# Seven PSUM banks as one tile, and the read-back of a unit's maxima issued nearer to its write, in an attention and gated-MLP block

## The chip, the cores and the metric

The kernel runs on one core of one Trainium2 chip. The metric is device time in microseconds (us) of one execution. A core has TensorE (PE; its weight loads are shown apart as PEld), VectorE (DVE), ScalarE (ACT), GpSimd (POOL) and SyncE (SP), each with its own in-order stream of instructions, and DMA queues. PSUM is the memory that matmuls write; here it is used as eight banks of 128 partitions by 512 fp32.

## The reference

Multi-query attention (32 query heads, one key and one value head of 16 dimensions) and a gated MLP follow each other on 2048 tokens of 512 features, each behind a layer norm and with a residual:

```python
def _A_ref(x, wq, wk, wv, wo):                    # B, S, D, H = 1, 2048, 512, 32; Dh = 16
    q = (x @ wq).reshape(B, S, H, Dh).transpose(0, 2, 1, 3)
    k = x @ wk
    v = x @ wv
    scores = jnp.einsum("bhqd,bkd->bhqk", q, k) * (Dh ** -0.5)
    p = _softmax(scores, axis=-1)
    o = jnp.einsum("bhqk,bkd->bhqd", p, v)
    return o.transpose(0, 2, 1, 3).reshape(B, S, H * Dh) @ wo
def _B_ref(x, W_gate, W_up, W_down):              # F = 1792
    gate, up = x @ W_gate, x @ W_up
    return (gate * (gate > 0) * up) @ W_down
h = x + _A_ref(_layernorm(x), A_wq, A_wk, A_wv, A_wo)
h2 = h + _B_ref(_layernorm(h), B_W_gate, B_W_up, B_W_down)
```

## The kernel before, in words

All is fp32. Where fp32 accuracy is wanted from single-pass matmuls, an operand is split into a rounded part and the rest, and three matmuls add up (`PASSES`, line 262).

Attention is cut into 32 units: 256 tokens of 8 heads each. A unit needs two sweeps over all keys. The first finds each row's maximum score: `max_mm` (line 611) makes one matmul of 512 columns into a bank (L619) and one VectorE reduction of that bank to 128 numbers (`mpart`, L621). A unit has 64 of them. `max_finish` (line 623) then takes the maximum, splits and transposes it, writes it to DRAM (`c_dram`, L638) and reads it back from there into two rows of the unit's queries (`qaug`, L642). The second sweep, `score_mm` (line 652), multiplies keys by these queries (L658), so that the maximum is subtracted on the way, and ScalarE takes exp of the bank into `p` (L661). `value_block` (line 665) multiplies probabilities by values into a bank of its own, "O" (L674); it waits for no B bank.

Layer norms, projections and the MLP are accumulation chains (`Chain`, line 268). Inside the attention each chain matmul is run as two halves of 64 rows (L297), which fill the PE array's rows between the attention's matmuls; a chain keeps one B bank from its first matmul to its last and is then read by ACT, by DVE or by both. The seven banks B0 to B6 are shared by all: `bank()` (line 190) asks the pool for a new tile with the tag of the bank that the planner has chosen, so each use of a bank is a tile of its own.

The order of all this on TensorE, and with it on all engines, is written out by hand: a string `ORDER` of letters (line 49), read by the loop that starts at line 1176. `m`/`M` is a `max_mm` on the lower or upper 64 rows, `e`/`E` a `score_mm`, `g`/`G` one half matmul of a chain, `O` a value block, `T` a turn (transposes). A planner of estimated clocks beside it chooses the bank and the time from which side work (`at`, line 207) is issued. In the program each matmul's reader is written down right behind the matmul, and only then comes the next matmul. The tile layer adds the waits: it records what each instruction reads and writes of each tile, and puts semaphore waits where it finds a conflict.

Of the kernel before, what the change touches and what calls it, by code (L numbers as in the profile page):

```python
# [16 lines left out]
S, D, H, DH, F = 2048, 512, 32, 16, 1792  # L17
# [9 lines left out]
STEPS = NB * 2  # L27
NP = 10
BANKS = [f"B{i}" for i in range(7)]
# [8 lines left out]
PASS, LOAD, SEEN, CHANGE, VALUE, BACK, TURN = 230, 107, 425, 95, 882, 237, 214  # L38

EXP, EXP_FREE, RED, RED_FREE, COPY, ADD, FREE = 494, 650, 600, 740, 541, 600, 150  # L40
ROUND, DIFF, PRODUCT, SCALE, HOP, ISSUE = 640, 1290, 1150, 640, 2600, 600
APPLY, LANDING, ASKED, SPREAD, RAW_LAG = 705, 4700, 5500, 5600, 1500


A_AT, V_AT, P_AT, QUERIES_AT, KEYS_AT, LN_AT = 1800, 1500, 3900, 0, 0, (0, 3000, 2500)

# [110 lines left out]
def block_kernel(ctx: ExitStack, tc: tile.TileContext, x, wq, wkv, wo, wgu, wd, out):  # L157
    nc = tc.nc
    pool = lambda name, **kw: ctx.enter_context(tc.tile_pool(name=name, bufs=1, **kw))
    consts = pool("consts")  # L160
    sb = pool("sb")
    ps = pool("ps", space=PSUM)
# [3 lines left out]
    ident = consts.tile([128, 128], F32, name="ident")  # L166
# [7 lines left out]
    kaug = consts.tile([128, S], F32R, name="kaug")  # L174
# [11 lines left out]


    rota = {"n": 0, "tags": []}

    def bank(tag=None):  # L190
        if tag is None:
            tag = rota["tags"][rota["n"] % len(rota["tags"])]
            rota["n"] += 1
        return ps.tile([128, 512], F32, name=tag, bufs=1)


    clk = {"A": 0.0, "V": 0.0, "P": 0.0, "S": 0.0}
# [388 lines left out]
    qaug = {}  # L586
# [21 lines left out]

    mpart = {}

    def max_mm(m, ab, tag):

        v, i = divmod(m, STEPS)
        j, p, c = i // 8, i // 4 % 2, i % 4
        if v not in mpart:
            mpart[v] = sb.tile([128, 2, 2, 4, 4], F32, name="mpart", bufs=2)
        r = slice(64 * ab, 64 * ab + 62)
        b = bank(tag)
        nc.tensor.matmul(b, qaug[v][r, p, c * 128:(c + 1) * 128], kaug[r, j * 512:(j + 1) * 512],  # L619
                         start=True, stop=True)  # L620
        nc.vector.tensor_reduce(mpart[v][:, ab, p, c, j:j + 1], b, axis=AX.X, op=ALU.max)  # L621

    def max_finish(v):

        m = sb.tile([128, 2, 8], F32, name="mfin", bufs=2)
        nc.vector.tensor_reduce(m.rearrange("p a n -> p (a n)"), mpart.pop(v).rearrange("p a q c j -> p (a q c) j"),
                                axis=AX.X, op=ALU.max)

        ms = sb.tile([128, 2, 2, 8], F32, name="msplit", bufs=2)
        nc.vector.tensor_copy(ms[:, :, 0].bitcast(F32R), m)  # L630
        nc.vector.tensor_tensor(ms[:, :, 1], m, ms[:, :, 0], op=ALU.subtract)

        mt = sb.tile([128, 32], F32, name="mturned", bufs=2)
        nc.vector.transpose(mt, ms.rearrange("p a l n -> p (a l n)"))
        t = on("V", 0.0, 950) + FREE

        def written():
            nc.sync.dma_start(out=c_dram[v], in_=mt)  # L638

        def landed():  # L640
            for ab in range(2):
                nc.sync.dma_start(out=qaug[v][64 * ab + 62:64 * ab + 64].bitcast(F32)  # L642
                                  .rearrange("l q (c i j) -> l (q c) i j", i=4, j=32),
                                  in_=c_dram[v].rearrange("(i a l n) j -> a l n i j", i=4, a=2, l=2)[ab])
            stamp["rows", v] = t + 2 * HOP

        at(t, written)
        at(t + HOP, landed)

    probs = {}  # L650

    def score_mm(g, ab, tag):

        v, i = divmod(g, STEPS)
        kb, p = divmod(i, 2)
        r = slice(64 * ab, 64 * ab + 64)
        b = bank(tag)
        nc.tensor.matmul(b, kaug[r, kb * 128:(kb + 1) * 128], qaug[v][r, p, :], start=True, stop=True)  # L658
        if g not in probs:
            probs[g] = sb.tile([128, 2, T], F32, name="p", bufs=NP)  # L660
        nc.scalar.activation(probs[g][:, ab], b, AF.Exp, scale=DH ** -0.5)  # L661

    obank, osb = {}, {}

# [242 lines left out]
    N = len(UNITS) * STEPS  # L907
# [16 lines left out]
    warm = bank("O")  # L924
# [118 lines left out]
    clk.update(A=A_AT, V=V_AT, P=P_AT, S=0.0)  # L1043
    stamp.update({("xnT", 0, k): 0.0 for k in range(KT)})
    stamp["key", 0], stamp["ln", 1] = KEYS_AT, LN_AT[0]
    end_o, end_t = None, False

    def normalise(t):
# [127 lines left out]
    while not done():  # L1176
# [33 lines left out]
        tag = next_bank() if free else None  # L1210
        starts = {}
        for k in range(2):
            g, w, c = ge[k], me[k], (low, high)[k]
            if g < N and ("rows", g // STEPS) in stamp and g - NP < 2 * on_ and tag:
                starts["eE"[k]] = place(k, max(stamp["rows", g // STEPS], bfree[tag]))
            if w < N and w // STEPS in qtime and w // STEPS <= maxed + 1 and tag and (
                    w >= STEPS or ("key", w // 8) in stamp):
                starts["mM"[k]] = place(k, max(qtime[w // STEPS], bfree[tag], stamp["key", w // 8] if w < STEPS else 0.0))
            if c is not None and (c.tag or tag):
                starts["gG"[k]] = place(k, max(c.t, 0.0 if c.tag else bfree[tag]) if c.i == 0 else 0.0)  # L1220
        top = max(lanes)
        if on_ < N // 2 and len(exps.get(2 * on_ + 1, ())) == 2:
            dep = max(max(exps[g].values()) for g in range(2 * on_, 2 * on_ + 2)) + FREE
# [26 lines left out]
        if any(x.ready() + CHANGE <= top and (x.ready() + 4000 < top or on_ == N // 2) for x in turns):  # L1250
            do_turns()
            continue
        letter = next(order)
        if letter == "T":
            if pending in turns:
                turns.remove(pending)
            for source in (fronts, feeds):
                if source.held is pending:
                    source.held = None
            turn_now(pending, tag, False, end_t)  # L1260
            continue
        kind, k = letter.upper(), int(letter.isupper())
        issued = s = starts[letter]
# [89 lines left out]
```

## Time and profile before

| | us |
|---|---|
| median of 3 runs (1733.37 to 1734.95) | 1734.67 |
| the profiled execution | 1735.53 |
| its span, from first to last instruction | 1733.8 |
| mean granted TensorE clock, share of full | 0.994 |

The profile gives, for one execution, the busy time of each engine, groups of equal instructions by source line (count, sum, mean in ns, idle time ahead of them and who ended it), the waits by pairs of engines, the timeline, and busy time and granted clock in chosen stretches. `B<-kaug,qaug` is a matmul that writes a bank B from `kaug` and `qaug`; the numbers of buffers are left out.

### The profile page before, as it was taken

To read this page: it belongs to the slowest core of one execution; us is meant where nothing else is said; L and a number is where in the kernel's file an instruction comes from. 1 tells how busy PE (TensorE), PEld (TensorE's weight loads), DVE (VectorE), ACT (ScalarE), POOL (GpSimd) and SP (SyncE) were. 2 spreads that over 40 slices of the span, in tenths; PEclk is the share of its full clock that TensorE was granted. 3 is DMA by queue.
4 is the path that set the end of the run, shared out by engine and by line. 5 is a ranking of instruction groups with operands and counts; after the bars stand their busy time and mean duration, and the time that the engine had idled before them with its cause. 6 is when DMAs were issued, how large, how long until landed. Compare 5 with 4: busy or idle time off the path is not lost.

```text
span 1733.8 us, 40138 instructions
## 1 busy us (share of the span) xinstructions
PE 1712.0 (99%) x15566; PEld 1141.9 (66%) x15566; DVE 1451.0 (84%) x2524; ACT 1251.2 (72%) x2488; POOL 854.0 (49%) x1015
## 2 busy tenths in 40 slices
PE   8999999999999999999999999999999999999999
PEld 6755334766656666666766667666666666666688
DVE  8899999988998888988888888897898888986266
ACT  7478977777777777777777777777767777778724
POOL 5511301666415656286544667276655557276410
PEclk9999999999999999999999999999999999999999
DMA  3323211332212222233222223232223223122343
GB/s 129 92 74 86 77 32 26 97 95 79 83 58 72 75 79 81 71 96 97 77 61 83 77 87 99 72 103 70 79 69 108 77 79 102 48 87 81 107 138 116
DMA packets 101970, 144.07 MB, mean 83 GB/s; under 512 B 27156, under 2 KB 39572, under 8 KB 101780
## 3 DMA queue, kind: packets, MB, share of 16 engines
q1 hardware_dynamic: 100724, 141.19, 27.4%
q8 instruction: 122, 2.00, 0.5%
q14 instruction: 68, 0.56, 0.1%
q10 hardware_dynamic: 1056, 0.33, 0.1%
HBM read 119.73 MB, written 21.49 MB: 81 GB/s over the span
## 4 chain that ended last, share of the span: by engine, by line
PE 93%; DVE 5%; issue 1%; DMA 1%; ACT 0%; POOL 0%; SPq 0%; POOLq 0%; DVEq 0%; ACTq 0%
PE B L297 27%; PE O L674 27%; PE B L658 16%; PE B L619 16%; PE B L288 4%; DVE mpart L621 4%; PE B L514 1%; PE O L926 1%; PE B L404 0%; DVE msplit L630 0%; PE B L1001 0%; DMA c_dram<-mturned 0%; DVE hn L397 0%; DMA qaug<-c_dram 0%; PE B L581 0%
## 5 line engine op out<-in xcount | busy, mean ns | idle before, releaser
L621 DVE TENSOR_REDUCE mpart<-B 128x1 f32<-128x512 f32 x2048 | 1268.8, 682 | 190.6 <-PE B L619 111.6
L661 ACT ACTIVATE p<-B 128x512 f32<-128x512 f32 x2048 | 1091.0, 606 | 359.8 <-PE B L658 200.3
L619 PE MATMUL B<-kaug,qaug 62*128 62x512 f32 x2048 | 746.6, 421 | 8.3 <-DVE hT L566 2.6
L658 PE MATMUL B<-qaug,kaug 64*128 64x512 f32 x2048 | 713.6, 417 | 5.6 <-DMA qaug<-c_dram 3.6
L297 PE MATMUL B<-hn,gu 64*128 64x256 f32 x4704 | 564.8, 282 | 0.0
L297 PEld LDWEIGHTS B<-hn,gu 64*128 64x128 f32 x4704 | 533.9, 186 | 24.6 <-issue 15.6
L674 PE MATMUL O<-p,vv 128*32 128x512 f32 x4096 | 510.4, 601 | 0.0
L619 PEld LDWEIGHTS B<-kaug,qaug 62*128 62x128 f32 x2048 | 348.3, 185 | 157.7 <-DVE mpart L621 52.7
L658 PEld LDWEIGHTS B<-qaug,kaug 64*128 64x128 f32 x2048 | 337.6, 186 | 164.7 <-DVE mpart L621 53.4
L869 POOL TENSOR_TENSOR hf<-hf,ga 128x256 f32<-128x256 f32 x92 | 67.4, 733 | 426.0 <-ACT hf L867 417.7
L297 PE MATMUL B<-wd,hT 64*128 64x512 f32 x1176 | 274.6, 395 | 0.1
L240 POOL TENSOR_TENSOR gu<-wraw,gu 128x512 fp32r<-128x512 f32 x195 | 252.9, 1297 | 16.3
L674 PEld LDWEIGHTS O<-p,vv 128*32 128x32 f32 x4096 | 99.8, 109 | 192.0 <-issue 175.5
L297 PEld LDWEIGHTS B<-wd,hT 64*128 64x128 f32 x1176 | 192.0, 185 | 15.3 <-issue 2.7
L240 POOL TENSOR_TENSOR wd<-wraw,wd 128x512 fp32r<-128x512 f32 x95 | 122.4, 1289 | 7.9
L239 POOL TENSOR_SCALAR gu<-wraw 128x512 fp32r<-128x512 f32 x195 | 120.8, 619 | 11.1 <-PE B L297 8.0
L297 PE MATMUL B<-wo,act 64*128 64x512 f32 x384 | 88.3, 394 | 0.1
L240 POOL TENSOR_TENSOR hT<-hf,hT 128x256 fp32r<-128x256 f32 x97 | 72.9, 752 | 8.1
L357 POOL TENSOR_TENSOR rs<-ve,nhalf 128x2 f32<-128x2 f32 (+1 forms) x13 | 10.2, 783 | 125.5 <-DVE nm L353 125.4
L861 ACT ACTIVATE ga<-B 128x256 f32<-128x256 f32 x112 | 43.5, 388 | 39.0 <-PE B L288 24.6
L297 PEld LDWEIGHTS B<-wo,act 64*128 64x128 f32 x384 | 62.6, 185 | 5.5 <-issue 1.7
L528 POOL TENSOR_TENSOR act<-raw,act 128x512 fp32r<-128x512 f32 x16 | 20.6, 1290 | 89.4 <-ACT raw L527 85.7
(134 smaller groups left out, 916.3 us busy)
## 6 DMA issues: line engine op xcount, KB each, us to landing
wraw<-wgu SPq DMA_DIRECT2D x224, 256.0 KB
wraw<-wd SPq DMA_DIRECT2D x112, 256.0 KB
q_dram<-act SPq DMA_DIRECT2D x32, 256.0 KB
qaug<-q_dram SPq DMA_DIRECT2D x62, 128.0 KB
o_dram<-osb SPq DMA_DIRECT2D x31, 256.0 KB
x<-x SPq DMA_DIRECT2D x16, 256.0 KB
out<-h SPq DMA_DIRECT2D x16, 256.0 KB
qaug<-q_dram SPq DMA_DIRECT2D x62, 64.0 KB
```

Of the source, the lines that this page charges most:

```text
L239: nc.gpsimd.tensor_scalar(dst[:, 0], src, 1.0, 0.0, op0=ALU.mult, op1=ALU.add)
L240: nc.gpsimd.tensor_tensor(dst[:, 1], src, dst[:, 0].bitcast(F32), op=ALU.subtract)
L288: nc.tensor.matmul(out(self.bank), l(a), r(b), start=i == 0, stop=i == len(self.ops) - 1)
L297: mm = nc.tensor.matmul(out(self.bank), l(a)[rows], r(b)[rows], start=opens and which == 0, stop=closes and which == 1)
L528: nc.gpsimd.tensor_tensor(qs[:, 1], q, qs[:, 0].bitcast(F32), op=ALU.subtract)
L619: nc.tensor.matmul(b, qaug[v][r, p, c * 128:(c + 1) * 128], kaug[r, j * 512:(j + 1) * 512], start=True, stop=True)
L621: nc.vector.tensor_reduce(mpart[v][:, ab, p, c, j:j + 1], b, axis=AX.X, op=ALU.max)
L658: nc.tensor.matmul(b, kaug[r, kb * 128:(kb + 1) * 128], qaug[v][r, p, :], start=True, stop=True)
L661: nc.scalar.activation(probs[g][:, ab], b, AF.Exp, scale=DH ** -0.5)
L674: nc.tensor.matmul(obank[v][32 * h:32 * h + 32], vv[:, kb, :], probs[g + p][:, ab], start=kb == 0, stop=kb == NB - 1)
L861: nc.scalar.activation(ga[:, :n], p[:, :n], AF.Relu)
L869: nc.gpsimd.tensor_tensor(hf[:, :n], hf[:, :n], ga[:, :n], op=ALU.mult)
```

## The change

Two things are changed that reach the program. The read-back of the maxima is due `ROWS_HOP` = 1700 planned nanoseconds behind the write, where it was `HOP` = 2600; the planned time of its landing stays 5200 (`ROWS_AT`, before 2 x `HOP`). And the seven B banks are one tile of 128 x 7 x 512, allocated once; `bank()` returns a slice of it. The rest adds letters that read two neighbouring banks with one instruction (`X`, `P`), a letter that waits (`W`), a way to finish maxima on GpSimd and warming matmuls: `POOL_ROWS` is 0, `WARMERS` is False, and `ORDER`, which is the same string in both, has none of the three letters, so none of this is in the program.

```diff
+ROWS_HOP, ROWS_AT = 1700, 5200
+POOL_ROWS = 0
+WARMERS = False
...
     rota = {"n": 0, "tags": []}
+    banks = ps.tile([128, len(BANKS), 512], F32, name="B", bufs=1)
...
-        return ps.tile([128, 512], F32, name=tag, bufs=1)
+        return banks[:, BANKS.index(tag)] if tag in BANKS else ps.tile([128, 512], F32, name=tag, bufs=1)
...
-    def max_mm(m, ab, tag):
+    def max_mm(m, ab, tag, pair=None):
...
+        for h in (ab, 1 - ab) if pair is not None else (ab,):
+            r = slice(64 * h, 64 * h + 62)
+            b = bank(tag) if pair is None else banks[:, pair + h]
+            nc.tensor.matmul(b, qaug[v][r, p, c * 128:(c + 1) * 128], kaug[r, j * 512:(j + 1) * 512],
+                             start=True, stop=True)
+        if pair is None:
+            nc.vector.tensor_reduce(mpart[v][:, ab, p, c, j:j + 1], b, axis=AX.X, op=ALU.max)
+        else:
+            nc.vector.tensor_reduce(mpart[v][:, :, p, c, j], banks[:, pair:pair + 2], axis=AX.X, op=ALU.max)
...
-            stamp["rows", v] = t + 2 * HOP
+            stamp["rows", v] = t + ROWS_AT
 
         at(t, written)
-        at(t + HOP, landed)
+        at(t + ROWS_HOP, landed)
```

The order of the instructions on PE, DVE, ACT and POOL is the same in both programs. What differs there is what they wait for.

On PE, in the middle of the program (a gate and up chain beside the two sweeps), before: L658 and L619 are the sweeps' matmuls, L297 the halves of a chain, the number behind B is the bank and the one behind _ the use of it.

```order
L297 MATMUL B2_10585<-hn_7613,gu_10085 128x256 x2
L658 MATMUL B6_10717<-qaug1_76,kaug_78 128x512 [waits DVE_49]
L297 MATMUL B2_10585<-hn_7612,gu_10088 128x256 x2
L619 MATMUL B5_10723<-kaug_78,qaug2_77 128x512 [waits Activation_49]
L297 MATMUL B2_10585<-hn_7612,gu_10088 128x256 x2
L658 MATMUL B0_10728<-qaug1_76,kaug_78 128x512 [waits DVE_49]
L297 MATMUL B2_10585<-hn_7612,gu_10088 128x256
L619 MATMUL B1_10733<-kaug_78,qaug2_77 128x512 [waits Activation_49]
L297 MATMUL B2_10585<-hn_7612,gu_10088 128x256
```

The same place now (L683 was L658, L627 was L619, L303 was L297):

```order
L683 MATMUL B_87<-qaug1_76,kaug_78 128x512
L303 MATMUL B_87<-hn_6261,gu_8348 128x256 [waits Activation_49]
L303 MATMUL B_87<-hn_6261,gu_8348 128x256
L627 MATMUL B_87<-kaug_78,qaug2_77 128x512
L303 MATMUL B_87<-hn_6261,gu_8348 128x256 [waits DVE_49]
L303 MATMUL B_87<-hn_6261,gu_8348 128x256
L683 MATMUL B_87<-qaug1_76,kaug_78 128x512
L303 MATMUL B_87<-hn_6261,gu_8348 128x256 [waits Activation_49]
L627 MATMUL B_87<-kaug_78,qaug2_77 128x512
L303 MATMUL B_87<-hn_6261,gu_8348 128x256 [waits DVE_49]
```

The wait has moved from the sweep's matmul, which waited for the last reader of its own bank, to the instruction behind it: the next chain matmul, in another bank, waits for ACT behind each score matmul and for DVE behind each maximum matmul. The counts that these waits compare with, in the two built programs, say for which instruction: before, 3916 of the 4555 waits of a matmul for an instruction of ACT or DVE name one that read a matmul 9 to 24 places back on PE; now 4093 of 4425 name the reader of the matmul one place back.

On DVE, in the middle of the program, before (the reductions of `mpart`; L893 adds a chain's bank to `h`):

```order
L621 TENSOR_REDUCE mpart_7827<-B6_8601 128x1 [waits PE_49]
L621 TENSOR_REDUCE mpart_7827<-B3_8610 128x1 [waits PE_49]
L621 TENSOR_REDUCE mpart_7827<-B0_8619 128x1 [waits PE_49]
L621 TENSOR_REDUCE mpart_7827<-B1_8631 128x1 [waits PE_49]
L621 TENSOR_REDUCE mpart_7827<-B3_8634 128x1 [waits PE_49]
L621 TENSOR_REDUCE mpart_7827<-B0_8645 128x1 [waits PE_49]
```

The same place now:

```order
L630 TENSOR_REDUCE mpart_6436<-B_87 128x1 [waits PE_49,Activation_49] x4
L630 TENSOR_REDUCE mpart_6436<-B_87 128x1 [waits PE_49]
L630 TENSOR_REDUCE mpart_6436<-B_87 128x1 [waits PE_49,Activation_49]
L921 TENSOR_TENSOR h_5875<-B_87,h_5875 128x512 [waits PE_49,Pool_49]
L630 TENSOR_REDUCE mpart_6436<-B_87 128x1 [waits PE_49,Activation_49] x2
```

A second wait, for ACT's last read of any bank, has come to 1039 of the 2048 reductions; the second of two waits stands in an instruction of its own ahead of the reduction (DVE has 1227 such instructions where it had 180, ACT 1505 where it had 940).

On SP, where unit 2's maxima are written and read back, before and now (in five other units it passes one or two transfers, in 26 none):

```order
L638 DMA c_dram<-mturned 128x32
L431 DMA wraw<-wo 128x1x512 x4
L431 DMA wraw<-wgu 128x512 x4
L642 DMA qaug_77<-c_dram 2x32x32 x2
L226 DMA q_dram<-act 8x16x512 x2
```

```order
L662 DMA c_dram<-mturned 128x32
L666 DMA qaug_77<-c_dram 2x32x32 x2
L437 DMA wraw<-wo 128x1x512 x4
L437 DMA wraw<-wgu 128x512 x4
L232 DMA q_dram<-act 8x16x512 x2
```

The read-back (L642, now L666) has moved ahead of eight loads of weights.

More of the change, by code (lines that the diff above doesn't have):

```diff
@@ L40 @@
 EXP, EXP_FREE, RED, RED_FREE, COPY, ADD, FREE = 494, 650, 600, 740, 541, 600, 150
+EXP_TWO, RED_TWO = 860, 1134
+ROWS_HOP, ROWS_AT = 1700, 5200
+POOL_ROWS = 0
+WARMERS = False
 ROUND, DIFF, PRODUCT, SCALE, HOP, ISSUE = 640, 1290, 1150, 640, 2600, 600
@@ L616, in max_mm @@
             mpart[v] = sb.tile([128, 2, 2, 4, 4], F32, name="mpart", bufs=2)
[L617 to L621, printed above, removed]
+        for h in (ab, 1 - ab) if pair is not None else (ab,):
[3 more added lines that the diff above has]
+                             start=True, stop=True)
@@ L623, in max_finish @@
+        if pair is None:
+            nc.vector.tensor_reduce(mpart[v][:, ab, p, c, j:j + 1], b, axis=AX.X, op=ALU.max)
+        else:
+            nc.vector.tensor_reduce(mpart[v][:, :, p, c, j], banks[:, pair:pair + 2], axis=AX.X, op=ALU.max)
     def max_finish(v):
         m = sb.tile([128, 2, 8], F32, name="mfin", bufs=2)
-        nc.vector.tensor_reduce(m.rearrange("p a n -> p (a n)"), mpart.pop(v).rearrange("p a q c j -> p (a q c) j"),
-                                axis=AX.X, op=ALU.max)
@@ L629, in max_finish @@
         ms = sb.tile([128, 2, 2, 8], F32, name="msplit", bufs=2)
-        nc.vector.tensor_copy(ms[:, :, 0].bitcast(F32R), m)
-        nc.vector.tensor_tensor(ms[:, :, 1], m, ms[:, :, 0], op=ALU.subtract)
+        part = mpart.pop(v).rearrange("p a q c j -> p (a q c) j")
+        flat = m.rearrange("p a n -> p (a n)")
+        if v < POOL_ROWS:
+            half = sb.tile([128, 16, 2], F32, name="mhalf", bufs=2)
+            nc.gpsimd.tensor_tensor(half, part[:, :, :2], part[:, :, 2:], op=ALU.max)
+            nc.gpsimd.tensor_tensor(flat, half[:, :, 0], half[:, :, 1], op=ALU.max)
+            nc.gpsimd.tensor_scalar(ms[:, :, 0].bitcast(F32R), m, 1.0, None, op0=ALU.mult)
+            nc.gpsimd.tensor_tensor(ms[:, :, 1], m, ms[:, :, 0], op=ALU.subtract)
+            t = on("P", clk["V"] + FREE, 1000) + FREE
+            at(t, lambda: max_turned(v, ms, on("V", t, 250) + FREE))
+        else:
+            nc.vector.tensor_reduce(flat, part, axis=AX.X, op=ALU.max)
+            nc.vector.tensor_copy(ms[:, :, 0].bitcast(F32R), m)
+            nc.vector.tensor_tensor(ms[:, :, 1], m, ms[:, :, 0], op=ALU.subtract)
+            max_turned(v, ms, on("V", 0.0, 950) + FREE)
@@ L633, in max_finish, with max_turned @@
+    def max_turned(v, ms, t):
         mt = sb.tile([128, 32], F32, name="mturned", bufs=2)
         nc.vector.transpose(mt, ms.rearrange("p a l n -> p (a l n)"))
-        t = on("V", 0.0, 950) + FREE
         def written():
@@ L644, in landed, with score_mm @@
                                   in_=c_dram[v].rearrange("(i a l n) j -> a l n i j", i=4, a=2, l=2)[ab])
-            stamp["rows", v] = t + 2 * HOP
+            stamp["rows", v] = t + ROWS_AT
         at(t, written)
-        at(t + HOP, landed)
+        at(t + ROWS_HOP, landed)
     probs = {}
-    def score_mm(g, ab, tag):
+    def score_mm(g, ab, tag, pair=None):
         v, i = divmod(g, STEPS)
         kb, p = divmod(i, 2)
-        r = slice(64 * ab, 64 * ab + 64)
-        b = bank(tag)
-        nc.tensor.matmul(b, kaug[r, kb * 128:(kb + 1) * 128], qaug[v][r, p, :], start=True, stop=True)
+        for h in (ab, 1 - ab) if pair is not None else (ab,):
+            r = slice(64 * h, 64 * h + 64)
+            b = bank(tag) if pair is None else banks[:, pair + h]
+            nc.tensor.matmul(b, kaug[r, kb * 128:(kb + 1) * 128], qaug[v][r, p, :], start=True, stop=True)
         if g not in probs:
             probs[g] = sb.tile([128, 2, T], F32, name="p", bufs=NP)
-        nc.scalar.activation(probs[g][:, ab], b, AF.Exp, scale=DH ** -0.5)
+        if pair is None:
+            nc.scalar.activation(probs[g][:, ab], b, AF.Exp, scale=DH ** -0.5)
+        else:
+            nc.scalar.activation(probs[g], banks[:, pair:pair + 2], AF.Exp, scale=DH ** -0.5)
     obank, osb = {}, {}
@@ L1045, in block_kernel @@
     stamp["key", 0], stamp["ln", 1] = KEYS_AT, LN_AT[0]
+    last_busy = 0.0
     end_o, end_t = None, False
@@ L1220, in block_kernel @@
                 starts["gG"[k]] = place(k, max(c.t, 0.0 if c.tag else bfree[tag]) if c.i == 0 else 0.0)
+        pair = min((i for i in range(len(BANKS) - 1) if BANKS[i] in free and BANKS[i + 1] in free),
+                   key=lambda i: max(bfree[BANKS[i]], bfree[BANKS[i + 1]]), default=None)
+        ahead = int(lanes[0] > lanes[1])
+        if pair is not None:
+            both = max(bfree[BANKS[pair]], bfree[BANKS[pair + 1]])
+            g, w = ge[0], me[0]
+            if ge[0] == ge[1] and g < N and ("rows", g // STEPS) in stamp and g - NP < 2 * on_:
+                starts["X"] = place(ahead, max(stamp["rows", g // STEPS], both))
+            if me[0] == me[1] and w < N and w // STEPS in qtime and w // STEPS <= maxed + 1 and (
+                    w >= STEPS or ("key", w // 8) in stamp):
+                starts["P"] = place(ahead, max(qtime[w // STEPS], both, stamp["key", w // 8] if w < STEPS else 0.0))
         top = max(lanes)
@@ L1253, in block_kernel @@
         letter = next(order)
+        if letter == "W":
+            lanes = [max(l, later[0][0]) for l in lanes]
+            continue
         if letter == "T":
@@ L1262, in block_kernel @@
         kind, k = letter.upper(), int(letter.isupper())
+        if on_ == 0 and WARMERS:
+            idle = starts[letter] - max(last_busy, max(lanes) - 6000.0)
+            if idle > 400:
+                warm = bank("O")
+                for _ in range(min(16, int((idle - 200) / 150))):
+                    nc.tensor.transpose(warm[:, :128], ident, ident)
+            last_busy = starts[letter] + PASS
+        if kind in "XP":
+            s = starts[letter]
+            issued = max(lanes[1 - ahead], s)
+            lanes[ahead], lanes[1 - ahead] = s + PASS, issued + PASS
+            end_o, end_t = None, False
+            if kind == "X":
+                score_mm(ge[0], ahead, None, pair)
+                e0 = max(clk["A"], issued + SEEN, oend.get(ge[0] - NP, 0.0))
+                clk["A"] = e0 + EXP_TWO
+                exps[ge[0]] = {0: clk["A"] + 100, 1: clk["A"] + 100}
+                ge = [ge[0] + 1] * 2
+                done_at = e0 + EXP_TWO + 156
+            else:
+                max_mm(me[0], ahead, None, pair)
+                r0 = max(clk["V"], issued + SEEN)
+                clk["V"] = r0 + RED_TWO
+                me = [me[0] + 1] * 2
+                done_at = r0 + RED_TWO + 140
+                if me[0] == (maxed + 1) * STEPS:
+                    max_finish(maxed)
+                    maxed += 1
+            bfree[BANKS[pair]] = bfree[BANKS[pair + 1]] = done_at
+            continue
         issued = s = starts[letter]
```

## The prediction

> **What bounds the kernel now.** The page comes first: busy times, clock, the chain that ended last, the costliest groups (busy us, mean ns of one | idle time before).
>
> ```profile
> span 1733.8 us, 40138 instructions
> PE 1712.0 (99%) x15566; PEld 1141.9 (66%) x15566; DVE 1451.0 (84%) x2524; ACT 1251.2 (72%) x2488; POOL 854.0 (49%) x1015
> ...
> PE 93%; DVE 5%; issue 1%; DMA 1%; ACT 0%; POOL 0%; SPq 0%; POOLq 0%; DVEq 0%; ACTq 0%
> ...
> L621 DVE TENSOR_REDUCE mpart<-B 128x1 f32<-128x512 f32 x2048 | 1268.8, 682 | 190.6 <-PE B L619 111.6
> L661 ACT ACTIVATE p<-B 128x512 f32<-128x512 f32 x2048 | 1091.0, 606 | 359.8 <-PE B L658 200.3
> L619 PE MATMUL B<-kaug,qaug 62*128 62x512 f32 x2048 | 746.6, 421 | 8.3 <-DVE hT L566 2.6
> L658 PE MATMUL B<-qaug,kaug 64*128 64x512 f32 x2048 | 713.6, 417 | 5.6 <-DMA qaug<-c_dram 3.6
> ```
>
> PE bounds it: 93% of the chain, hardly idle. DVE (84%) and ACT (72%) read 4096 banks beside it. That three engines are busy at once rests on the seven banks: PE is some banks ahead of its readers. The view of waits shows how little is lost (us, times, longest):
>
> ```profile
> PEld B L658 <- DVE mpart L621: 53.4, 79, 2.3
> PEld B L619 <- DVE mpart L621: 52.7, 75, 2.0
> ...
> PE B L658 <- DMA qaug<-c_dram: 3.6, 2, 1.9
> ```
>
> **The read-back.** In six of 32 units it moves ahead of one to eight transfers. PE waited for it twice, 3.6 us in all: a gain of 0 to 3.6 us. What it is moved past lands up to one issue later. I take 0, since the next part stretches the time between write and use.
>
> **One tile.** It removes no instruction of an engine and adds about 1,750 waiting ones. What matters is what they name: the rows in the section on the change, with their counts, say that 4093 times a matmul waits for the reader of the matmul just ahead, in another bank. PE takes its instructions in order, so a wait at the head of its stream holds everything behind it: the chain matmuls, which need no reader at all, and the next sweep's matmul, whose bank has long been free. ACT and DVE, whose next work is that matmul's, idle in turn. Six of the seven banks then wait empty, and the kernel becomes one chain: matmul, reader, matmul, reader. The value blocks alone, in a bank of another tile, can pass beside a reader. Its 4096 links I price from the timeline (start, duration, what ended the idle time):
>
> ```profile
> 27.45 1.88 DVE L621 TENSOR_REDUCE mpart<-B 128x1 f32<-128x512 f32 x3
> 28.19 1.33 PE L619 MATMUL B<-kaug,qaug 62*128 62x512 f32 x3 [1.72 <-DVE mpart L621]
> ...
> 84.24 0.50 PE L619 MATMUL B<-kaug,qaug 62*128 62x512 f32 x1 [0.59 <-ACT raw L527]
> 84.78 0.69 DVE L621 TENSOR_REDUCE mpart<-B 128x1 f32<-128x512 f32 x1 [0.40 <-PE B L619]
> ...
> 87.55 0.46 PE L658 MATMUL B<-qaug,kaug 64*128 64x512 f32 x1 [1.90 <-DMA qaug<-c_dram]
> 88.05 0.60 ACT L661 ACTIVATE p<-B 128x512 f32<-128x512 f32 x1 [1.29 <-PE B L658]
> ```
>
> The first reduction ends at 27.45 + 0.68 = 28.13, and the matmul that waited for it starts at 28.19: 0.06 from reader to matmul. A matmul that found PE idle starts its reader 84.78 - 84.24 = 0.54 later (0.50 for the score matmul; I take 0.54). The readers take 0.68 and 0.60. So at full clock a maximum link is 0.06 + 0.54 + 0.68 = 1.28, a score link 1.20, and 2048 of both 5079 us: three times the present span.
>
> **The clock** decides the size. PE's busy time and the granted clock (eighth column of numbers, PEclk), in stretches that follow the clock's own changes:
>
> ```profile
> core 0: us, PE busy (x) PEld busy (x) DVE busy (x) ACT busy (x) POOL busy (x), PEclk, DMA share, GB/s
> 23.54:26.95 3.41, 2.74 (x15) 1.56 (x12) 2.65 (x8) 3.04 (x8) 1.88 (x2) 1.00 0.00 0
> 26.95:30.36 3.41, 1.50 (x4) 0.66 (x4) 3.41 (x6) 2.95 (x9) 1.45 (x3) 1.00 0.01 2
> 30.36:33.78 3.42, 1.54 (x6) 0.69 (x5) 3.42 (x7) 3.36 (x9) 1.20 (x2) 0.50 0.01 2
> 84.98:88.39 3.41, 1.51 (x14) 1.04 (x14) 1.68 (x3) 1.42 (x3) 1.91 (x2) 1.00 0.21 27
> 88.39:91.80 3.41, 3.41 (x20) 3.15 (x18) 1.60 (x3) 1.46 (x3) 0.00 (x0) 0.50 0.51 177
> 255.64:259.06 3.42, 1.50 (x5) 0.78 (x5) 3.42 (x7) 0.00 (x0) 0.00 (x0) 1.00 0.26 85
> 259.06:262.47 3.41, 3.18 (x13) 1.56 (x15) 2.03 (x5) 3.35 (x7) 0.00 (x0) 0.50 0.05 4
> 262.47:265.88 3.41, 3.41 (x19) 1.20 (x14) 2.04 (x5) 1.47 (x4) 0.00 (x0) 0.50 0.71 172
> 265.88:269.29 3.41, 3.36 (x26) 1.20 (x25) 2.56 (x6) 3.14 (x7) 1.28 (x1) 1.00 0.55 138
> 1665.35:1668.76 3.41, 1.81 (x12) 1.42 (x13) 2.68 (x7) 1.21 (x4) 0.00 (x0) 1.00 0.42 131
> 1668.76:1672.17 3.41, 3.41 (x18) 3.41 (x17) 0.01 (x1) 0.00 (x0) 0.00 (x0) 0.50 0.85 284
> ```
>
> The clock has two values. It was halved behind each stretch of 3.41 us in which PE was busy 1.81 or less, and kept behind 2.74. It came back behind a stretch that was busy throughout (262.47), and not behind 1.54 or 3.18 (30.36, 259.06). In the new chain PE is busy 0.50 of each 1.28 us in bare links, 1.3 of 3.41: far under the mark; and once the clock is halved, bare links hold PE busy about half of the time, which doesn't bring it back. So I take half clock for all but the stretches that PE fills.
>
> What a link costs then, and the other terms:
>
> ```profile
> 259.77 0.79 PE L658 MATMUL B<-qaug,kaug 64*128 64x512 f32 x1 [0.23 <-ACT p L661]
> ...
> 88.75 0.62 PE L619 MATMUL B<-kaug,qaug 62*128 62x512 f32 x1
> ...
> 699.13 1.92 PE L674 MATMUL O<-p,vv 128*32 128x512 f32 x16
> ...
> 261.97 1.93 PE L674 MATMUL O<-p,vv 128*32 128x512 f32 x8
> ...
> 704.70 0.42 ACT L861 ACTIVATE ga<-B 128x256 f32<-128x256 f32 x1
> 704.96 0.43 ACT L867 ACTIVATE hf<-B 128x256 f32<-128x256 f32 x1
> ...
> 702.04 0.40 PE L297 MATMUL B<-hn,gu 64*128 64x256 f32 x2
> ...
> 702.26 0.42 PE L658 MATMUL B<-qaug,kaug 64*128 64x512 f32 x1
> 702.28 0.40 PE L297 MATMUL B<-hn,gu 64*128 64x256 f32 x2
> ```
>
> At half clock a lone matmul takes 0.79 for 0.50, one behind others 0.62 for 0.40 (702.04). The terms, full clock and half clock, in us; counts are along PE's order in the built program:
>
> - 2048 pairs of links: 5079; with 0.29 more for each of 4096, 6267.
> - The waiting instructions ahead of some 1,640 readers, where the second wait is the one already met: between 0 and the 0.07 by which such starts scatter (nothing in the trace has a second wait for a reader); 80 in both.
> - Chain matmuls stand between links, no longer beside readers. Two of 256 columns pass in 702.28 - 702.04 = 0.24, so 0.12 each (0.23 for 512), two halves side by side: summed over the gaps between links, 545; 1090.
> - In 1940 links such work runs ahead of the sweep's matmul, which then takes 0.40 for 0.50 (0.62 for 0.79): -194; -330.
> - 512 value blocks of 8 recorded matmuls, 1.92 / 2 = 0.96 each at full clock, 1.93 at half (261.97). 308 of them follow a chain matmul or another block and add in full: 296; 594. 204 follow a sweep's matmul directly and lie beside its reader: nothing; at half clock they outlast it, 0.42 + 1.93 against a link of 1.53 on average: 169.
> - Some 250 chains and turns close with readers that the next matmul now awaits: 0.06, the last matmul about 0.4, and the two reads, 704.70 to 705.39, so about 1.2; 1.5: 300; 375.
> - Before the first and behind the last link: 35; 45.
>
> The sums are 6141 at full clock and 8290 at half. There are 120 places with two or more value blocks in a row (3.9 us and more at half clock); perhaps 80 fill a stretch and bring the clock back for some 5 us, in which a third of the time is saved: 80 x 5 x 0.35 = 140. **Span 8150 us**; the profiled execution lay 1735.5 - 1733.8 = 1.7 above its span and 0.9 above the median, which is nothing here. The pieces of a link are good to 3%, so this case's own range is 7800 to 8500.
>
> What hid the readers before was the other six banks; that cover is gone. POOL, SP and DMAs get four times the time for the same work, and are late nowhere.
>
> **The rivals.**
>
> *The clock stays full:* 6140 us. No gap in a link is longer than 0.68 + 0.06 and the 0.04 between matmul and reader, 0.78; if only longer gaps count, the clock stays. The Trainium skill ("TensorE: Matmul & The Clock Gate", Part 1: The HAM clock gate) lets the clock fall after an idle window of some 3.4 us, and asks for no gap over about 3 us between bursts; by that rule the clock would stay up, and the sum be the one for full clock. The trace speaks against this case: in 84.98 to 88.39 the longest gap was the 1.90 ahead of 87.55, and the clock fell. 8%.
>
> *The clock goes to and fro:* half of the work at either clock, (6141 + 8290) / 2 = 7200. It needs a mark for coming back that partly idle stretches reach. The Trainium skill (the same title, "A second HAM failure mode: psum-queue depth-cycling") reports such oscillation where banks are cycled with short idles. The stretch at 259.06, busy 3.18 and still not raised, speaks against. 9%.
>
> *Not slower:* the named waits are met before PE comes to them, and the read-back gains its 3.6: 1731 to 1735. That needs readers that end before the next matmul could start. A reader starts 0.50 behind its matmul at the earliest and takes 0.60, PE's next start is 0.12 to 0.23 behind: only if the waits were not those in the rows. The price decides from the point where the wait is longer than PE's own work ahead of it. 5%, 2% of it faster by over 0.2%.
>
> *Longer links:* if each of the added waits cost its 0.07 on both sides, or a halved clock slowed more than PE's rows show, 8290 + 400 = 8700 and more. 4%.
>
> **How the numbers follow.** The chain at half clock has 74%. The range from 7200 to 8700 leaves out full clock, no slowdown, the lower half of the to and fro, and a few above: 2 in 10. Within 0.2%, about what a measurement of this kernel can tell from no change: 3%; faster 2%; slower 95%.
>
> **What would show it.** Right: PE's idle time goes from 1% to about half, ended by DVE `mpart` and ACT `p`; the chain of waits shares itself between PE, DVE and ACT; DVE's and ACT's busy sums stay near 1451 and 1251; the clock is near 0.5 in nearly every slice; value blocks directly behind a sweep's matmul start without a wait. Wrong: a clock of 1.0 in slices that are half idle, or PE starting matmuls of several banks before the first is read.

## The result, and the profile after

The changed kernel takes **8109.51 us** (median of four runs, 8109.16 to 8110.05), the kernel before 1734.02 (1732.52 to 1734.95) beside it: a ratio of 4.677, 95% interval 4.669 to 4.685. The profiled execution spans 8107.9 us.

From the page of the changed kernel: the busy sums, the slices of PE and of the granted clock, the chain of work that ended last, and five of the costliest groups.

```profile
span 8107.9 us, 41882 instructions
...
PE 4910.6 (61%) x15566; PEld 2130.0 (26%) x15566; DVE 1605.1 (20%) x2524; ACT 1406.7 (17%) x2488; POOL 845.5 (10%) x1015
...
PE   5666666556566555656566555665655665556667
...
PEclk6555555555555555555555555555555555555557
...
PE 61%; DVE 18%; ACT 16%; issue 4%; DVEq 0%; ACTq 0%; DMA 0%; POOL 0%; POOLq 0%
...
L630 DVE TENSOR_REDUCE mpart<-B 128x1 f32<-128x512 f32 x2048 | 1416.1, 691 | 6026.6 <-PE B L627 5964.3
L303 PE MATMUL B<-hn,gu 64*128 64x256 f32 x4704 | 1495.5, 482 | 1315.8 <-DVE mpart L630 670.6
L687 ACT ACTIVATE p<-B 128x512 f32<-128x512 f32 x2048 | 1223.2, 597 | 5978.3 <-PE B L683 5951.0
L683 PE MATMUL B<-qaug,kaug 64*128 64x512 f32 x2048 | 1541.7, 753 | 621.9 <-DVE mpart L630 364.8
L627 PE MATMUL B<-kaug,qaug 62*128 62x512 f32 x2048 | 1489.8, 727 | 458.8 <-ACT p L687 218.2
```

PE was busy 99% of 1733.8 us and is now busy 61% of 8107.9. Its busy sum went from 1.7 ms to 4.9 with the same 15,566 recorded matmuls, because the clock shows 5 in nearly every slice and most matmuls start behind an idle PE. The other 39% are waits. The chain goes round PE, DVE and ACT, which before was PE's alone; DVE and ACT do their old work, one instruction at a time, and sit idle for some 6 ms each, waiting for a sweep's matmul. The view of the waits says the same from the other side; its columns are the sum in us, the number of times and the longest.

```profile
DVE mpart L630 <- PE B L627: 5964.3, 2015, 12.6
ACT p L687 <- PE B L683: 5951.0, 2031, 13.3
...
PE B L303 <- DVE mpart L630: 1028.0, 1218, 1.3
PE B L303 <- ACT p L687: 947.5, 1345, 1.1
```

One stretch of its timeline (start, duration, then in brackets the idle time ahead and what ended it):

```profile
3301.02 0.60 ACT L687 ACTIVATE p<-B 128x512 f32<-128x512 f32 x1 [2.96 <-PE B L683]
...
3301.67 0.80 PE L303 MATMUL B<-wo,act 64*128 64x512 f32 x2 [0.69 <-ACT p L687]
...
3302.26 0.62 PE L683 MATMUL B<-qaug,kaug 64*128 64x512 f32 x1
3302.92 0.60 ACT L687 ACTIVATE p<-B 128x512 f32<-128x512 f32 x1 [1.31 <-PE B L683]
...
3303.57 1.22 PE L303 MATMUL B<-wo,act 64*128 64x512 f32 x3 [0.69 <-ACT p L687]
...
3305.63 0.79 PE L627 MATMUL B<-kaug,qaug 62*128 62x512 f32 x1 [0.84 <-DVE h L850]
...
3306.36 1.94 PE L702 MATMUL O<-p,vv 128*32 128x512 f32 x8
3306.46 0.69 DVE L630 TENSOR_REDUCE mpart<-B 128x1 f32<-128x512 f32 x1
```

No reader of a B bank lies beside a matmul, except beside the value block at 3306.36, which goes to O and waits for no B bank. The exp that starts at 3302.92 ends at 3303.52; the chain's matmul for another bank starts 0.05 later. The matmul of 3305.63 has its reader at 3306.46, 0.83 behind.

### The profile page after: what moved, and what is told of

It reads as the page before. It is cut to its first block, busy times and chain, and to the rows that moved or that the text cites. A ratio compares the mean times of both kernels' runs of the same rounds, so it can differ in the third digit from the quotient of the medians.

```text
span 8107.9 us, 41882 instructions
## 1 busy us (share of the span) xinstructions
PE 4910.6 (61%) x15566; PEld 2130.0 (26%) x15566; DVE 1605.1 (20%) x2524; ACT 1406.7 (17%) x2488; POOL 845.5 (10%) x1015
## 4 chain that ended last, share of the span: by engine, by line
PE 61%; DVE 18%; ACT 16%; issue 4%; DVEq 0%; ACTq 0%; DMA 0%; POOL 0%; POOLq 0%
PE B L303 25%; DVE mpart L630 17%; ACT p L687 15%; PE B L683 12%; PE B L627 11%; PE O L702 11%; PE B L294 1%; DVE h L921 1%; ACT ga L889 0%; ACT hf L895 0%; DVEq L630 0%; PE B L520 0%; PE B L410 0%; PE B L587 0%; ACT hn L397 0%
## 5 line engine op out<-in xcount | busy, mean ns | idle before, releaser
L630 DVE TENSOR_REDUCE mpart<-B 128x1 f32<-128x512 f32 x2048 | 1416.1, 691 | 6026.6 <-PE B L627 5964.3
L303 PE MATMUL B<-hn,gu 64*128 64x256 f32 x4704 | 1495.5, 482 | 1315.8 <-DVE mpart L630 670.6
L687 ACT ACTIVATE p<-B 128x512 f32<-128x512 f32 x2048 | 1223.2, 597 | 5978.3 <-PE B L683 5951.0
L683 PE MATMUL B<-qaug,kaug 64*128 64x512 f32 x2048 | 1541.7, 753 | 621.9 <-DVE mpart L630 364.8
L627 PE MATMUL B<-kaug,qaug 62*128 62x512 f32 x2048 | 1489.8, 727 | 458.8 <-ACT p L687 218.2
L303 PEld LDWEIGHTS B<-hn,gu 64*128 64x128 f32 x4704 | 968.3, 303 | 1985.6 <-DVE mpart L630 946.2
L303 PE MATMUL B<-wd,hT 64*128 64x512 f32 x1176 | 669.4, 721 | 471.8 <-ACT p L687 238.5
L683 PEld LDWEIGHTS B<-qaug,kaug 64*128 64x128 f32 x2048 | 577.4, 282 | 1271.1 <-DVE mpart L630 603.0
L702 PE MATMUL O<-p,vv 128*32 128x512 f32 x4096 | 908.7, 1017 | 0.0
L627 PEld LDWEIGHTS B<-kaug,qaug 62*128 62x128 f32 x2048 | 593.6, 290 | 987.6 <-ACT p L687 374.4
L303 PEld LDWEIGHTS B<-wd,hT 64*128 64x128 f32 x1176 | 268.0, 290 | 813.6 <-ACT p L687 351.8
L303 PE MATMUL B<-wo,act 64*128 64x512 f32 x384 | 210.4, 701 | 151.0 <-ACT p L687 70.9
L303 PEld LDWEIGHTS B<-wo,act 64*128 64x128 f32 x384 | 85.0, 280 | 266.0 <-ACT p L687 122.0
```

Of the source, the lines that this page charges most:

```text
L303: mm = nc.tensor.matmul(out(self.bank), l(a)[rows], r(b)[rows], start=opens and which == 0, stop=closes and which == 1)
L702: nc.tensor.matmul(obank[v][32 * h:32 * h + 32], vv[:, kb, :], probs[g + p][:, ab], start=kb == 0, stop=kb == NB - 1)
```

## The experiments

The theory: every matmul into the seven-bank tile waits for the reader of the matmul ahead, whatever bank that one used, and every reader for the reader ahead; this makes one chain of matmul and reader, and since PE then does too little in a given time, its clock halves. The rivals: the moved read-back, the tile as such (its place in PSUM), the waits without the clock.

### The two halves of the change, each alone

Read-back alone:

```diff
-    banks = ps.tile([128, len(BANKS), 512], F32, name="B", bufs=1)
...
-        return banks[:, BANKS.index(tag)] if tag in BANKS else ps.tile([128, 512], F32, name=tag, bufs=1)
+        return ps.tile([128, 512], F32, name=tag, bufs=1)
```

> The seven banks are seven tiles again; the read-back keeps its new place (ROWS_HOP = 1700), so this is that half of the change alone. Theory (the waits between banks of one tile are everything): 4555 matmul waits as before, 14 of them on the reader of the matmul one place back, so 1731 to 1735 us. Rival (SP, which now issues six of the units' read-backs ahead of other transfers, holds up loads): well above 1735, PE's idle time ended by DMA. PE busy 99%, clock 1.0 in nearly all slices.

Measured: 1733.83 us against 1733.44, ratio 1.0004 (0.9996 to 1.0013), clock 0.994. PE's waits for the read-back in this kernel:

```profile
PE B L682 <- DMA qaug<-c_dram: 1.9, 1, 1.9
```

Before there were two of them, 3.6 us in all. One of the two is gone, and the 1.7 us that it frees can't be told from the scatter of the runs.

One tile alone:

```diff
-ROWS_HOP, ROWS_AT = 1700, 5200
+ROWS_HOP, ROWS_AT = 2600, 5200
```

> Seven banks as one tile, the read-back where it was (ROWS_HOP = 2600). Theory: the same 4093 waits on the reader one place back as in the changed kernel, so 8110 us within 0.3% (8085 to 8135), clock near 0.53. Rival (the two halves of the change work together): visibly less than 8100.

Measured: 8112.42 us (8109.10 to 8113.65), ratio 4.680 (4.674 to 4.686), clock 0.532. The tile is the whole of it, and the two halves don't act together.

### One tile without the waits

A tile of eight banks, with O as the eighth, has no added waits in the program that is built. Why the layer that sets the waits tells banks of this tile apart, and not those of the seven-bank tile, was not found; in a built program with the seven banks laid out as [128, 3584] the same 4093 waits stand (it was not timed). For the experiment it is enough that this program joins the banks into one tile as the changed kernel does, and has the matmul waits of the kernel before (14 on the reader one place back).

```diff
-    banks = ps.tile([128, len(BANKS), 512], F32, name="B", bufs=1)
+    banks = ps.tile([128, 8, 512], F32, name="B", bufs=1)
...
-        return banks[:, BANKS.index(tag)] if tag in BANKS else ps.tile([128, 512], F32, name=tag, bufs=1)
+        return banks[:, (BANKS + ["O"]).index(tag)]
```

> One tile again, but of eight banks: O is its eighth place, nothing else differs from the changed kernel. In the built program the matmul waits are the 4555 of before, 14 of them on the reader one place back (the seven-bank tile: 4093). Theory (the named waits are what costs, not that banks share a tile): 1731 to 1735 us, within 0.2% of the read-back alone, clock 1.0. Rival (banks of one tile are slower in themselves, by addresses or by how the engines reach them): near 8110 us, or at the least over 1800.

Measured: 1733.21 us, ratio 0.9996 (0.9987 to 1.0006). The busy sums and the clock on its page:

```profile
span 1733.0 us, 40130 instructions
...
PE 1711.9 (99%) x15566; PEld 1140.9 (66%) x15566; DVE 1449.5 (84%) x2524; ACT 1250.7 (72%) x2488; POOL 854.3 (49%) x1015
...
PEclk9999999999999999999999999999999999999999
```

One tile costs nothing by itself. The waits, and the clock that follows from them, are the whole cost.

### Fewer banks to a tile

The same edit each time, with other groups of banks:

```diff
-    banks = ps.tile([128, len(BANKS), 512], F32, name="B", bufs=1)
+    GROUPS = [[0, 1], [2], [3], [4], [5], [6]]
+    blocks = [ps.tile([128, len(g), 512], F32, name=f"B{n}", bufs=1) for n, g in enumerate(GROUPS)]
...
+        for block, g in zip(blocks, GROUPS):
+            if tag in BANKS and BANKS.index(tag) in g:
+                return block[:, g.index(BANKS.index(tag))]
```

> Banks B0 and B1 are one tile of two, the other five are tiles of their own; read-back as in the changed kernel. In the built program 219 matmul waits name the reader one place back and 297 more the one two or three places back. Theory (each such wait costs what it costs in the changed kernel, 8110 - 1734 = 6376 us for 4079 of them, 1.56 us each, at half clock; without halved clock about (6141 - 1734) / 4079 = 1.08): 205 x 1.08 = 220 us at the least, and about 1.5 times the waits counted, 500 x 1.56 = 780, at the most: 1950 to 2500 us, clock kept at 1.0 in most slices since PE stays busy above the mark. Rival (any tile of several banks serialises the whole chain): 6000 and more. Rival (nothing below seven banks costs): 1734.

> Four tiles: B0 and B1, B2 and B3, B4 and B5, and B6 alone. In the built program 626 matmul waits name the reader one place back, 684 more two or three places back (one shared pair: 219 and 297, and 2554 us). Theory (time goes with the number of such waits, and the clock falls once they leave PE busy too little): by the shared pair's 820 us for 502 added waits, 1.63 each, 1296 x 1.63 = 2110 and 3850 us with its clock of 0.96; more if the clock falls: 3600 to 4400, granted clock between 0.6 and 0.9. Rival (only the reader one place back costs): 612 x 1.56 = 955, 2690.

> Two tiles: B0 to B3 and B4 to B6. 1752 matmul waits name the reader one place back, 1231 more two or three places back. Theory: between the tiles of two and the one tile, with the clock about as low as in the one tile (below 0.65), since PE is idle half of the time: 5500 to 6700. Rival (halving the sharing halves the cost): (1734 + 8110) / 2 = 4920.

| tiles | waits on the reader one place back | two or three back | us | ratio, 95% | clock |
|---|---|---|---|---|---|
| seven of one bank | 14 | 84 | 1733.8 | 1.000 to 1.001 | 0.994 |
| one of two banks, five of one | 219 | 297 | 2554.0 | 1.471 to 1.478 | 0.961 |
| three of two, one of one | 626 | 684 | 4188.8 | 2.410 to 2.420 | 0.652 |
| one of four, one of three | 1752 | 1231 | 6209.3 | 3.573 to 3.587 | 0.551 |
| one of seven | 4093 | 26 | 8109.5 | 4.669 to 4.685 | 0.532 |

The times follow the waits and the clock. The tiles of two and the two tiles came out inside their expected ranges. The shared pair came out at 2554, above its expected 1950 to 2500: the waits were counted as at most 502 more, but others cost as well (PE waited 662 times for `mpart` or `p` by the view of its waits). One stretch of that kernel's timeline shows what such a wait can do:

```profile
360.38 2.48 DVE L635 TENSOR_REDUCE mpart<-B 128x1 f32<-128x512 f32 x4 [0.74 <-PE B L688]
...
362.91 0.50 PE L688 MATMUL B<-qaug,kaug 64*128 64x512 f32 x2 [2.15 <-DVE mpart L635]
...
363.45 1.08 ACT L692 ACTIVATE p<-B 128x512 f32<-128x512 f32 x2 [2.52 <-PE B L688]
...
363.69 0.69 DVE L635 TENSOR_REDUCE mpart<-B 128x1 f32<-128x512 f32 x1 [0.83 <-PE B L632]
```

Five banks are still tiles of their own, so DVE and ACT run behind PE with several readers queued (four reductions in a row here, 2.48 us). A wait on the newest of them is a wait for the whole queue: PE starts again 0.05 us behind the end of the fourth, having idled for 2.15. By then the queue is empty, and ACT and DVE wait for PE in turn (2.52 and 0.83). The 662 waits come to 480 us; 446 of them, with 371 us, ended with a reader that had run directly behind another instruction of its engine. In the changed kernel 15 of 3,887 did.

A needless wait therefore costs no less here than in the serial chain. By the count of the expectation it is (2554 - 1734) / 502 = 1.63 us against 1.56. That count takes off the 14 of before, but not the 84 that name the reader two or three places back; with both taken off it is 820 / 418 = 1.96 for the shared pair, 2.03 for the tiles of two, 1.55 for the two tiles and 1.59 for the one tile. The 1.96 is at a clock of 0.961, where the prediction's sum for full clock would make it about 1.08.

### The clock

The waits were left as they are and PE's gaps filled, with matmuls that wait for nothing new: behind each sweep's matmul one in full float32, on the rows that the sweep uses, with zeros as weights, added to the open sums in O (3,699 of the 4,096 links have one; at the others O is closed). First of 384 columns, then of 128 (`COLS`):

```diff
+    zeros = consts.tile([128, 32], F32, name="zeros")
+    nc.vector.memset(zeros, 0.0)
...
+    COLS = 384
+
+    def keep_busy(at, rhs):
+
+        for o in obank.values():
+            nc.tensor.matmul(o[at:at + 32, :COLS], zeros[at:at + 62], rhs[at:at + 62, :COLS].bitcast(F32), start=False, stop=False)
...
             nc.tensor.matmul(b, qaug[v][r, p, c * 128:(c + 1) * 128], kaug[r, j * 512:(j + 1) * 512],
                              start=True, stop=True)
+            keep_busy(r.start, kaug[:, j * 512:(j + 1) * 512])
...
             nc.tensor.matmul(b, kaug[r, kb * 128:(kb + 1) * 128], qaug[v][r, p, :], start=True, stop=True)
+            keep_busy(r.start, qaug[v][:, p, :])
```

> The changed kernel with TensorE kept busy while the readers run: behind each sweep's matmul one more matmul of 384 columns in full float32 with zeros as its weights, which adds nothing to the open sums in O and waits for nothing new (3,699 of the 4,096 links have one; the others lie where O is closed). All waits of the changed kernel stay. From a value block (four of 512 columns in 0.96) one may take 0.72 at full clock, so it lies beside the reader (0.40 + 0.72 = 1.12 of a link of 1.28), and at half clock it fills PE (0.62 + 1.44 = 2.06 of 1.57), which should bring the clock back. Theory (a third of the changed kernel's 6376 us is the halved clock, and the clock follows PE's busy time): clock near 1.0 and 6141 + 196 for the value blocks that no longer lie beside a reader + some 200 for the links without one = 6550, between 6200 and 6900, faster than the changed kernel with 3,699 matmuls more. Rival (the clock falls for the waits, not for idle time): clock stays near 0.53, and PE's 2.06 sets the link: 8110 + 3699 x 0.5 = 9900. Rival (the clock does not set the time): 8110.

> As the one with 384 columns, but 128 columns (0.24 at full clock by the same row, 0.48 at half), so the same 3,699 matmuls fill a third of the gap. Theory (the clock comes back only behind a stretch of 3.41 us in which PE is busy throughout): at half clock PE is busy 0.79 + 0.48 of 1.57, 0.81 of the stretch, so the clock stays near 0.53 and the time at 8110 within 2% (7950 to 8270). Rival (any added busy time raises the clock in proportion): about a third of the way to the kernel with 384 columns, 7600.

Measured: 9814.62 us with 384 columns, clock 0.562; 8198.87 with 128, clock 0.535. With 384 the theory missed and its first rival came within 1% of the number. The rival's sum holds, since PE alone now sets the link (2.13 us from one sweep's matmul to the next, for its 2.06):

```profile
4000.92 0.79 PE L693 MATMUL B<-qaug,kaug 64*128 64x512 f32 x1
4001.64 1.48 PE L624 MATMUL O<-qaug,zeros 62*32 62x384 f32 x2
4003.05 0.79 PE L636 MATMUL B<-kaug,qaug 62*128 62x512 f32 x1
```

Its reason, that the clock falls for the waits, does not hold: the last run of this section keeps all the waits at a clock of 0.930. With 128 the time lay in the expected range, but the expectation stood on the same rule as the theory that missed with 384, so the hit says nothing for that rule.

From the view by stretches (length, then busy time and number of PE, PEld, DVE, ACT, POOL; the last three columns are clock, DMA share and GB/s), two of 3.41 us at half clock and one of 20 us in which the clock was full:

```profile
4000.00:4003.41 3.41, 3.41 (x6) 0.74 (x4) 0.37 (x1) 0.60 (x1) 0.00 (x0) 0.50 0.00 0
4003.41:4006.82 3.41, 3.41 (x6) 0.64 (x5) 1.38 (x2) 0.00 (x0) 0.00 (x0) 0.50 0.00 0
...
3870.00:3890.00 20.00, 19.40 (x82) 6.66 (x82) 4.84 (x7) 4.18 (x7) 0.00 (x0) 1.00 0.14 46
```

PE is busy without a gap and the clock stays halved. That is the end of the rule on which the theory stood, that a stretch that is busy throughout brings the clock back: of the 2,109 such stretches at half clock in this execution 103 were followed by full clock. In the changed kernel itself the rule looked right: 75 of 76.

What was tried next is a weight for each matmul: its cycles at full clock (one for each column, two for each record in float32), times the part of TensorE that it takes: half for 64 rows, a quarter for one of the four side by side of a value block, and for the added ones half, as for any on one half of the rows, though they give 32 columns. It is summed over each stretch of 3.41 us between possible steps of the clock and divided by the 8192 cycles that the stretch holds at full clock (at half clock, matmuls of 512 columns on all rows start 0.427 us apart in the changed kernel, so 4096 columns pass in 3.41 us). Over the 17,268 such stretches of the eleven executions profiled in this case, the clock of the next stretch was full where the weight was 3/8 or more and half where it was less, whichever it was before, with 94 exceptions (0.5%). If the added matmuls are weighed by rows and columns, an eighth each, there are over 1,500 exceptions: within these runs it is the rows that count.

By that measure one matmul on half of the rows is worth at most 0.25 at half clock, however busy PE is; at full clock it is worth up to 0.5 and may hold the clock, as in the 20 us of the third row above, where chain matmuls stand between. The weights and the mark were chosen on the stretches of the runs so far, so a kernel was run whose result they had to foretell (its stretches are among the 17,268): two of the added matmuls side by side.

```diff
-    def keep_busy(at, rhs):
+    def keep_busy(rhs):
...
-            nc.tensor.matmul(o[at:at + 32, :COLS], zeros[at:at + 62], rhs[at:at + 62, :COLS].bitcast(F32), start=False, stop=False)
+            for at in (0, 64):
+                nc.tensor.matmul(o[at:at + 32, :COLS], zeros[at:at + 62], rhs[at:at + 62, :COLS].bitcast(F32), start=False, stop=False)
...
-            keep_busy(r.start, kaug[:, j * 512:(j + 1) * 512])
+            keep_busy(kaug[:, j * 512:(j + 1) * 512])
...
-            keep_busy(r.start, qaug[v][:, p, :])
+            keep_busy(qaug[v][:, p, :])
```

> As the kernel that fills the gaps with one matmul of 384 columns of zeros as weights, but with two side by side, one on rows 0 to 63 and one on rows 64 to 127 (7,398 of them in all). Why: over the runs so far each stretch of 3.41 us, weighed by cycles of full clock and by the share of TensorE's rows that its matmuls use (a matmul on 64 rows counts half), was followed by full clock where the weight was above 3/8 and by half clock where it was below, with few exceptions, at either clock. One half-height matmul can't pass 0.25 at half clock however busy PE is; two side by side reach 0.36 in bare links, more where chains stand between, so the clock comes back within some stretches, and at full clock the links then weigh (0.107 + 0.64) / 1.28 = 0.58, so it stays. Theory (the clock goes by the part of TensorE that works): granted clock 0.9 or more and the chain's sum at full clock, 6141 + 196 for the value blocks that no longer lie beside a reader + some 200 for links without added matmuls = 6550 us, between 6200 and 7200. Rival (matmuls with zeros as weights, or of 32 columns, don't count): clock near 0.56 and 9815 us, as with one. Rival (the clock does not set the time): at clock 1.0 still 8100.

Measured: **6694.69 us** (6688.51 to 6702.69), clock 0.930, as the weight had it: 1415 us less than the changed kernel, with 7,398 matmuls more, and 3120 less than with half of them. From its page and its timeline:

```profile
PEclk6699999899999989999999999999999999989999
```

```profile
3003.63 0.50 PE L637 MATMUL B<-kaug,qaug 62*128 62x512 f32 x1
3004.06 0.84 PE L625 MATMUL O<-kaug,zeros 62*32 62x384 f32 x4
3004.91 0.50 PE L694 MATMUL B<-qaug,kaug 64*128 64x512 f32 x1
3005.34 0.83 PE L625 MATMUL O<-qaug,zeros 62*32 62x384 f32 x4
3006.10 0.50 PE L637 MATMUL B<-kaug,qaug 62*128 62x512 f32 x1
```

A sweep's matmul takes 0.50 again, and links follow at 1.28 (3003.63 to 3004.91) and 1.19, the first just as the prediction had it for full clock. All waits are still there. So of the 6375 us that the change costs, some 4,400 to 4,960 are the waits at full clock (6141 by the prediction's sum, 6695 by this run, each less 1734), and the rest is the clock that the waits bring down.

## Why the prediction was right, point by point

8150 was forecast from 7200 to 8700; 8109.5 was measured.

- *The links.* The prediction had 0.06 from reader to matmul, 0.83 from a lone matmul to its reader at half clock, and 0.68 or 0.60 for the reader. The trace after has 0.05, 0.83, 0.69 and 0.60: 2048 x (2 x 0.88 + 1.29) = 6246 for 6267.
- *The waiting instructions.* Taken at 80 between bounds of 0 and 0.07 each. What they cost depends on which wait stands ahead. Where the reader's own instruction carries the wait for ACT, and the wait for its matmul stands in the instruction ahead, the time from matmul to reader at half clock is 0.90 by the median for 989 reductions and 0.89 for 295 exps, against 0.83: 1284 x 0.06 = 77. Where the reader carries the wait for its matmul, and the one ahead is for DVE (742 exps), it is 0.83, and the instruction ahead costs nothing.
- *The clock in the changed kernel.* Near 0.5 in nearly all slices, as predicted; it was full for 515 us in 99 places, where the prediction allowed 80 places of 5 us. 92 of the 99 have value blocks in more than half of the 3.41 us ahead of them. If the time at full clock is put back at the ratio of the two sums, 8108 + 515 x (8290 / 6141 - 1) = 8288, for the sum of 8290. That is closer than the terms are known, so the last per cent of it is luck.
- *The clock's rule.* Right in its outcome and wrong as a rule, which happened to give the same clock here. "It came back behind a stretch that was busy throughout" holds in the changed kernel because there only value blocks, which use all rows, and chain matmuls in pairs fill a stretch; with 384 columns added on half of the rows it does not hold. The mark between 1.81 and 2.74 us of busy time has the same fault. The trace of before could hardly tell the two apart, since its stretches short of work were nearly all short of busy time too; the one at 259.06, busy for 3.18 of 3.41 us and not followed by full clock, was read as not busy throughout.
- *DVE's and ACT's busy sums.* Predicted to stay near 1451 and 1251; they are 1605.1 and 1406.7. An instruction takes the same 0.69 and 0.60, but before they ran one behind the other and overlapped a little in the records (2048 reductions of 682 ns in 1268.8 us), and now each stands alone (1416.1). It is no cost in the chain.
- *The value blocks.* As predicted those that follow a sweep's matmul directly lie beside its reader (3306.36 above). What the single terms for chain matmuls, value blocks and the ends of chains came to was not measured apart; only their total is borne out.
- *The read-back.* Predicted at nothing, at most the 3.6 us that PE waited for it: 1.0004 of the time, by itself.
- *The rivals.* Full clock, 6140, is what the chain comes near when the clock is held (6695 with 0.930 and the links without added matmuls). The Trainium skill ("TensorE: Matmul & The Clock Gate", Part 1: The HAM clock gate) lets the clock fall after an idle window; the trace disagrees, since PE's waits for a reader were 1.3 us at the longest in the rows above, and the clock was halved in 2,222 of its 2,372 stretches of 3.41 us. To and fro happened 98 times, but with 515 us of 8108 at full clock it decided little. *Not slower* is what the eight-bank tile does.

## What to carry to other kernels

Before banks or buffers are joined into one tile, look at which instruction each wait names in the program as built: a count of waits on the reader one place back (14 before, 4093 after) told what the busy times of the engines could not. A needless wait costs a whole round of matmul, reader and release, and it can empty the queues that the other buffers had filled: two of seven banks sharing a tile already cost 47%. When a chain leaves PE underused, its clock is a second loss on top, and what counted for it here was how many of the array's rows worked, not how long PE was busy.

## What the runs showed of the hardware that was not expected

- The granted clock followed the share of TensorE's rows in use, at both clocks by one mark near 3/8 of full work in a stretch of 3.41 us (94 exceptions in 17,268 stretches). PE busy in all of 2,109 stretches at half clock did not bring it back in 2,006 of them, and by that measure matmuls on 64 rows one at a time are worth a quarter there.
- Two matmuls side by side on the two halves of the rows made the kernel 3120 us faster than one: 6694.69 against 9814.62.
- Matmuls with zeros as weights counted for the clock as others on the same rows did: with them it rose to 0.930.
